# The gates of chunks 2 to 5 moved from the end of the opening to the middle of chunk 0

## The chip, the cores and the metric

The kernel runs on one core of a Trainium2 chip. The metric is the device time of one execution in microseconds (us); the median of a kernel's runs is what is compared. A profile is of one further execution, and gives its span: the time from the first to the last instruction.

## The reference

An mLSTM layer (a recurrent attention with an input, a forget and an output gate) over 4 batches of 8 heads, 768 positions and 40 values a head is followed by a gated feed-forward network of 320 inputs, 1536 inner columns and 320 outputs on the 3072 tokens. All is float32.

```
for t in range(S):                                   # 768 positions
    m_new  = max(f_gate[t] + m, i_gate[t])
    f_stab = exp(f_gate[t] + m - m_new); i_stab = exp(i_gate[t] - m_new)
    C = f_stab * C + i_stab * outer(v[t], k[t]); n = f_stab * n + i_stab * k[t]
    y[t] = sigmoid(o_gate[t]) * (C @ q[t]) / max(|n . q[t]|, 1)
x   = y as [4 * 768, 8 * 40]
out = (sigmoid(x @ w_gate) * (x @ w_val)) @ w_out
```

## The kernel before, in words

The 768 positions are six chunks of 128. A unit is one chunk of one batch (all 8 heads), so there are 24 units, (c, b). Inside a chunk the recurrence is written as attention: a unit's decay tile `d` of 128 x 8 x 128 is loaded from a small scratch row in DRAM, spread over the partitions (L219), turned into exponentials on ScalarE (L226, eight pieces, one for each head, in chunks 0 and 1), masked on POOL (L235), multiplied with the scores `s` (L427) and then with the values (`av`, L452). From chunk to chunk the state `cst` is carried: `in` (L447) reads it, `cs` (L500) adds to it through ScalarE copies (L512) and two VectorE sums (L517). The unit's result is divided by its denominator (L454 to L477) and transposed into `xh` and `xl`, the high and low parts of the feed-forward input of its chunk.

**Gates.** The gates of all 32 rows (batch times head) are rows of 768 numbers on 32 partitions. `gates_of(c0, c1)` makes the sums and maxima of chunks c0 to c1-1, all on VectorE: a running sum of the forget gates that starts anew in each chunk (L184), a difference (L185), for each chunk a running maximum `mg` and the value `mend` carried to the next chunk (L171, L172), and a last difference (L189). After each maximum SyncE stores `mg` to the scratch row `mscr` of its chunk (L173). Chunk 0's gates stand at the head of the opening and chunk 1's a little later in it; the call `gates_of(2, NCH)`, event g1, is for chunks 2 to 5: eleven VectorE operations (L184, L185 and L189 on 32 x 512, four L171 on 32 x 128, four tiny L172) and four stores. What they make is turned by TensorE: event h1 transposes the differences (`ptg`, four small L195) and VectorE copies them out as `at` (L197); event k1 transposes the last difference (`ptg` again), ScalarE takes its exponential `dec` (L199), and one more matmul and three VectorE operations spread it as `cdec` (L207 to L213).

**Feed-forward.** A tile (c, j, t0, t1) is inner column block j (12 of 128 columns) on 128 x (t1 - t0) tokens of chunk c. Its float32 products are made of high and low parts: 16 matmuls `pg` (L532 to L537) give gate and value in two PSUM tiles; then tanh on ScalarE (`sg`, L539), the product on VectorE (L540), a copy `gh` on ScalarE (L543), the remainder `gl` on VectorE (L544); the down matmuls `po` (L554 to L556) run one tile later. In chunk 0 the blocks 0 to 3 are done first on two batches, then on the other two (256 columns each), and blocks 4 to 11 on all four (512 columns).

**Weights.** They arrive as 64-bit words and are decoded during chunk 0, block by block: ScalarE (L259), VectorE (L264, L265, L269, tile `dc`), a high part on ScalarE (`wh` L294, `w` L297, `oh` L299) and a low part on POOL (`wl` L304, `w` L308, `ol` L310). SyncE issues nearly every load in one queue, in the program's order.

**Order.** Every step has a number in a table, `pos`; steps are recorded in the order of these numbers, and a feed-forward tile has its place in units of one full tile, so that 4.6 is shortly after block 4 of chunk 0. The framework's scheduler then orders each engine's instructions under the dependencies. Two things bind it: events of kind g, h and k are `pinned`, that is ordered behind the opening's last instruction on each engine; and `tc.issue_after(ins)` orders an engine's following instructions behind `ins`. PSUM tiles of the attention part share two banks of tag "pa": a tile that is to take a bank waits until the one before it there was read.

## Time and profile before

| | |
|---|---|
| runs | 572.92, 571.94, 572.35 us; median 572.35 |
| span of the profiled execution | 569.9 us; the median of the runs is 2.45 us above it, and the page gives no other time for the profiled execution |
| TensorE matmul busy | 546.7 us (96%), 3587 matmuls |
| VectorE / ScalarE / POOL busy | 319.5 us (56%) / 232.2 us (41%) / 162.2 us (28%) |
| DMA | 72.27 MB, mean 127 GB/s |

In the page's rows PE is TensorE, PEld its weight loads, DVE VectorE, ACT ScalarE, SP SyncE. In a list by time, the columns are start, time until the last of the group ended, engine, line, operation, output<-inputs, shape, count, and in brackets how long the engine had been idle and what ended that. A list of waits has engine and line, what it waited for, microseconds in total, times, longest. A table of windows has the window, its length, busy time of PE, PEld, DVE, ACT and POOL with counts, the granted TensorE clock (1.00 is full speed), the DMA engines' mean busy share and what they moved in GB/s.

### The profile page before, as it was taken

To read this page: it belongs to the slowest core of one execution; us is meant where nothing else is said; L and a number is where in the kernel's file an instruction comes from. 1 tells how busy PE (TensorE), PEld (TensorE's weight loads), DVE (VectorE), ACT (ScalarE), POOL (GpSimd) and SP (SyncE) were. 2 spreads that over 40 slices of the span, in tenths; PEclk is the share of its full clock that TensorE was granted. 3 is DMA by queue.
4 is the path that set the end of the run, shared out by engine and by line. 5 is a ranking of instruction groups with operands and counts; after the bars stand their busy time and mean duration, and the time that the engine had idled before them with its cause. 6 is when DMAs were issued, how large, how long until landed. Compare 5 with 4: busy or idle time off the path is not lost.

```text
span 569.9 us, 9906 instructions
## 1 busy us (share of the span) xinstructions
PE 546.7 (96%) x3587; PEld 497.0 (87%) x3587; DVE 319.5 (56%) x739; ACT 232.2 (41%) x581; POOL 162.2 (28%) x231
## 2 busy tenths in 40 slices
PE   8667999999999999999999999999999999999997
PEld 7565988788899999998888888888888888999996
DVE  5788878895755645555555544545543545432322
ACT  5285657754443442352243241433342332232322
POOL 5567646575420241311322310332210210000000
PEclk9789999999999999999999999999999999999999
DMA  9797747242674947354666544685644824010000
GB/s 197 193 240 185 202 123 192 93 115 54 169 173 119 183 103 182 100 147 125 167 125 156 132 141 129 149 171 124 140 125 134 206 56 121 4 47 2 24 2 23
DMA packets 131641, 72.27 MB, mean 127 GB/s; under 512 B 103113, under 2 KB 120777, under 8 KB 131593
## 3 DMA queue, kind: packets, MB, share of 16 engines
q1 hardware_dynamic: 130504, 71.39, 50.6%
q8 instruction: 28, 0.46, 0.3%
q10 hardware_dynamic: 1088, 0.26, 0.2%
q14 instruction: 21, 0.16, 0.1%
HBM read 56.95 MB, written 14.68 MB: 126 GB/s over the span
## 4 chain that ended last, share of the span: by engine, by line
PE 85%; DVE 7%; ACT 3%; issue 2%; POOL 2%; POOLq 0%; DVEq 0%; ACTq 0%
PE pg L532 34%; PE po L554 7%; PE po L556 7%; PE po L555 7%; PE av L452 6%; PE pg L534 6%; PE pg L537 6%; PE in L447 2%; PE s L434 2%; PE pt L373 2%; PE xt L488 2%; PE cs L500 2%; PE s L426 1%; DVE dc L264 1%; ACT d L226 1%
## 5 line engine op out<-in xcount | busy, mean ns | idle before, releaser
L539 ACT ACTIVATE sg<-pg 128x256 f32<-128x256 f32 (+1 forms) x103 | 48.3, 469 | 174.3 <-PE pg L537 174.2
L540 DVE SCALAR_TENSOR_TENSOR sg<-sg,pg 128x256 f32<-128x256 f32 (+1 forms) x103 | 53.9, 524 | 113.9 <-ACT sg L539 110.6
L532 PE MATMUL pg<-xh,wl 128*128 128x256 f32 (+1 forms) x412 | 111.1, 342 | 1.2 <-POOL wl L304 1.2
L532 PE MATMUL pg<-xh,wh 128*128 128x256 f32 (+1 forms) x412 | 110.9, 343 | 0.4 <-DVE sg L540 0.4
L532 PE MATMUL pg<-xl,wh 128*128 128x256 f32 (+1 forms) x412 | 108.7, 339 | 0.0
L556 PE MATMUL po<-oh,gl 128*128 128x320 f32 x288 | 93.0, 323 | 0.0
L554 PE MATMUL po<-oh,gh 128*128 128x320 f32 x288 | 92.3, 321 | 0.4 <-ACT gh L543 0.4
L555 PE MATMUL po<-ol,gh 128*128 128x320 f32 x288 | 92.4, 321 | 0.0
L544 DVE TENSOR_TENSOR gl<-sg,gh 128x256 fp32r<-128x256 f32 (+1 forms) x103 | 59.6, 579 | 35.5 <-ACT gh L543 34.9
L532 PEld LDWEIGHTS pg<-xh,wl 128*128 128x128 f32 x412 | 70.9, 191 | 8.5 <-POOL wl L304 1.4
L532 PEld LDWEIGHTS pg<-xh,wh 128*128 128x128 f32 x412 | 70.9, 191 | 5.8 <-DVE sg L540 0.6
L532 PEld LDWEIGHTS pg<-xl,wh 128*128 128x128 f32 x412 | 69.3, 190 | 6.6
L543 ACT ACTIVATE gh<-sg 128x256 fp32r<-128x256 f32 (+1 forms) x103 | 51.7, 502 | 47.7 <-DVE sg L540 47.7
L554 PEld LDWEIGHTS po<-oh,gh 128*128 128x128 f32 x288 | 54.5, 189 | 2.0 <-ACT gh L543 0.6
L555 PEld LDWEIGHTS po<-ol,gh 128*128 128x128 f32 x288 | 54.4, 189 | 1.3
L556 PEld LDWEIGHTS po<-oh,gl 128*128 128x128 f32 x288 | 54.2, 188 | 0.5 <-DVE gl L544 0.2
L534 PE MATMUL pg<-xh,w 128*128 128x256 f32 (+1 forms) x206 | 52.9, 332 | 0.7 <-POOL v L139 0.4
L537 PE MATMUL pg<-xl,w 128*128 128x256 f32 (+1 forms) x206 | 53.1, 331 | 0.0
L452 PEld LDWEIGHTS av<-v,d 128*128 128x128 f32 x352 | 46.8, 191 | 2.2 <-DVE d L427 0.6
L452 PE MATMUL av<-v,d 128*128 128x41 f32 x352 | 45.5, 269 | 0.4 <-DVE d L427 0.3
L508 POOL TENSOR_TENSOR cst<-cst,cdec 120x246 f32<-120x246 f32 (+1 forms) x32 | 16.0, 519 | 98.9 <-PE in L447 98.9
L235 POOL TENSOR_SCALAR_AFFINE_SELECT d<-d 128x1024 f32<-128x1024 f32 x22 | 24.2, 1101 | 50.1 <-ACT d L230 46.0
(128 smaller groups left out, 834.5 us busy)
## 6 DMA issues: line engine op xcount, KB each, us to landing
d<-mscr SPq DMA_DIRECT2D x22, 512.0 KB
ks<-scr SPq DMA_DIRECT2D x16, 360.0 KB
qs<-scr SPq DMA_DIRECT2D x16, 360.0 KB
k<-in_k_dram SPq DMA_DIRECT2D x24, 160.0 KB
v<-in_v_dram SPq DMA_DIRECT2D x24, 160.0 KB
o<-in_o_gate_dram SPq DMA_DIRECT2D x24, 160.0 KB
st_o<-in_moe_w_out_dram SPq DMA_DIRECT2D x12, 320.0 KB
out_dram<-ob SPq DMA_DIRECT2D x24, 160.0 KB
```

Of the source, the lines that this page charges most:

```text
L235: nc.gpsimd.affine_select(out=d, in_=d, pattern=[[0, H], [1, L]], compare_op=ALU.is_ge, fill=0.0, base=0, channel_multiplier=-1)
L452: nc.tensor.matmul(pv[:, h, :], dm[u][:, h, :], vt[u][:, h, :], start=True, stop=True)
L532: nc.tensor.matmul(pg[n], w[n][:, a, fs], x[c][:, a, n0:n1], start=(i + a == 0), stop=False)
L534: nc.tensor.matmul(pg[n], w2[n][:, fs], xh[c][:, 2, n0:n1], start=False, stop=False)
L537: nc.tensor.matmul(pg[n], w2[n][:, fs], xl[c][:, 2, n0:n1], start=False, stop=True)
L539: nc.scalar.activation(sg, pg[0], AF.Tanh, scale=0.5)
L540: nc.vector.scalar_tensor_tensor(sg, sg, 1.0, pg[1], ALU.add, ALU.mult)
L543: last = nc.scalar.activation(gh[u][:, :nt], sg, AF.Copy)
L544: E('gl0' if c == 0 else 'gl').tensor_tensor(gl[u][:, :nt], sg, gh[u][:, :nt].bitcast(F32), ALU.subtract)
L554: nc.tensor.matmul(po[t], g1[:, ts], oh[:, j, :], start=(j == 0), stop=False)
L555: nc.tensor.matmul(po[t], g1[:, ts], ol[:, j, :], start=False, stop=False)
L556: nc.tensor.matmul(po[t], g0[:, ts], oh[:, j, :], start=False, stop=(j == NF - 1))
```

## The change

The number of event g1 goes from 0.599 to 4.6, and its instructions are bound behind the VectorE remainder (`gl`, L544) of the feed-forward tile recorded last, here block 4 of chunk 0. Nothing is added to or taken from the computation.

```
-        ... 'w29': 13.171, 'g1': 0.599, 'h1': 5.3, 'k1': 5.5, ...
+        ... 'w29': 13.171, 'g1': 4.6, 'h1': 5.3, 'k1': 5.5, ...
@@ ffn_up
-        E('gl0' if c == 0 else 'gl').tensor_tensor(gl[u][:, :nt], sg, gh[u][:, :nt].bitcast(F32), ALU.subtract)
-        return last
+        lastv = E('gl0' if c == 0 else 'gl').tensor_tensor(gl[u][:, :nt], sg, gh[u][:, :nt].bitcast(F32), ALU.subtract)
+        return last, lastv
@@ emit
-            last = ffn_up(*tiles[kk])
+            last, lastv = ffn_up(*tiles[kk])
...
-                gates_of(2, NCH)
+                with tc.issue_after(lastv.ins):
+                    gates_of(2, NCH)
```

The scheduler makes of it the following orders. In the rows the running maxima and sums (L171, L184) are listed as SCALAR_TENSOR_TENSOR; `gin` is the tile of both gates, `dc_0_405` and `dc_1_415` are output weight blocks 0 and 1 in decoding.

VectorE at the end of the opening, before (L184, L185, three L171 and three L172 stand in a row ahead of this piece):

```order
L264 TENSOR_SCALAR dc_0_405<-dc_0_405 128x320
L171 SCALAR_TENSOR_TENSOR mg<-gin,mend 32x128
L264 TENSOR_SCALAR dc_1_415<-dc_1_415 128x320
L265 TENSOR_SCALAR dc_0_405<-dc_0_405 128x320
L265 TENSOR_SCALAR dc_1_415<-dc_1_415 128x320
L269 SCALAR_TENSOR_TENSOR dc_0_405<-st_o_139,dc_0_405 128x320
L269 SCALAR_TENSOR_TENSOR dc_1_415<-st_o_382,dc_1_415 128x320
L197 COPY at<-ptg_2_453 128x32
L172 TENSOR_TENSOR mend<-gin,mg 32x1
L189 TENSOR_TENSOR gin<-mend,mg 32x512
L540 SCALAR_TENSOR_TENSOR sg_0_0_474<-sg_0_0_474,pg_0_0_0_457 128x256
```

and now, directly behind the second unit's `xl`:

```order
L491 TENSOR_TENSOR xl_344<-xt_1_359,xh_343 128x3x128
L264 TENSOR_SCALAR dc_0_405<-dc_0_405 128x320
L265 TENSOR_SCALAR dc_0_405<-dc_0_405 128x320
L264 TENSOR_SCALAR dc_1_415<-dc_1_415 128x320
L269 SCALAR_TENSOR_TENSOR dc_0_405<-st_o_139,dc_0_405 128x320
L265 TENSOR_SCALAR dc_1_415<-dc_1_415 128x320
L197 COPY at<-ptg_2_453 128x32
L269 SCALAR_TENSOR_TENSOR dc_1_415<-st_o_382,dc_1_415 128x320
L540 SCALAR_TENSOR_TENSOR sg_0_0_474<-sg_0_0_474,pg_0_0_0_457 128x256
```

The eleven gate operations are gone from here; the decoding and the copy `at` of chunk 1's gates follow `xl` at once.

VectorE in the middle of chunk 0, from the remainder of block 4 to that of block 5, before (`o_0_398`, `t_1_0` and `x_0` belong to unit (1, 0); `dc_6_1230` is output weight block 6):

```order
L544 TENSOR_TENSOR gl_4_0_1045<-sg_4_0_1041,gh_4_0_1044 128x512
L265 TENSOR_SCALAR dc_3_1185<-dc_3_1185 128x256
L265 TENSOR_SCALAR dc_6_1230<-dc_6_1230 128x320
L454 TENSOR_TENSOR t_1_0_1053<-t_1_0_1053,av_0_1055 128x328
L269 SCALAR_TENSOR_TENSOR dc_3_1185<-st_3_911,dc_3_1185 128x256
L467 TENSOR_SCALAR den_0_1065<-t_1_0_1053 128x8
L471 SCALAR_TENSOR_TENSOR o_0_398<-o_0_398,t_1_0_1053 128x320
L468 SCALAR_TENSOR_TENSOR den_0_1065<-t_1_0_1053,den_0_1065 128x8
L269 SCALAR_TENSOR_TENSOR dc_6_1230<-st_o_929,dc_6_1230 128x320
L469 RECIPROCAL den_0_1065<-den_0_1065 128x8
L477 TENSOR_TENSOR x_0_1070<-o_0_398,den_0_1065 128x320
L540 SCALAR_TENSOR_TENSOR sg_5_0_1123<-sg_5_0_1123,pg_0_5_0_1106 128x512
```

Behind that piece stood L197, the copy `at`. Now, the later part of the same stretch (ahead of it, from `gl_4` on, stand L184, L185, two L171 and two L172, the unit's denominator and `x`, and the two L517):

```order
L171 SCALAR_TENSOR_TENSOR mg<-gin,mend 32x128
L540 SCALAR_TENSOR_TENSOR sg_5_0_1123<-sg_5_0_1123,pg_0_5_0_1106 128x512
L172 TENSOR_TENSOR mend<-gin,mg 32x1
L197 COPY at<-ptg_6_1130 128x128
L171 SCALAR_TENSOR_TENSOR mg<-gin,mend 32x128
L359 COPY qk_1_1136<-pt_1_1_1143 120x256
L172 TENSOR_TENSOR mend<-gin,mg 32x1
L544 TENSOR_TENSOR gl_5_0_1127<-sg_5_0_1123,gh_5_0_1126 128x512
L189 TENSOR_TENSOR gin<-mend,mg 32x512
L362 TENSOR_TENSOR qbd_1_1137<-qk_1_1136,bmask 80x256
L264 TENSOR_SCALAR dc_6_1230<-dc_6_1230 128x320
```

The gates are threaded between the unit's operations, and the decoding of block 6 has moved from both sides of `gl_4` to behind L189.

TensorE at the same place, before (`po_0_914` and `po_0_915` are the outputs of batches 2 and 3; `pt_1_1_1148` is the third transposed piece of unit (1, 1), `ptg_6_1174` the second turning of the gates):

```order
L357 MATMUL pt_1_1_1143<-ident,k_1_555 120x128
L556 MATMUL po_0_914<-oh,gl_4_0_1045 128x320
L554 MATMUL po_0_915<-oh,gh_4_0_1044 128x320
L555 MATMUL po_0_915<-ol,gh_4_0_1044 128x320
L556 MATMUL po_0_915<-oh,gl_4_0_1045 128x320
L357 MATMUL pt_1_1_1148<-ident,q_1_554 80x128
L357 MATMUL pt_1_1_1148<-ident,k_1_555 80x128
L532 MATMUL pg_0_6_0_1196<-xh_343,wh_98 128x512
L195 MATMUL ptg_6_1174<-ident,gin 128x32 x4
```

and now (the same tiles, with the outputs called 899 and 900):

```order
L357 MATMUL pt_1_1_1148<-ident,q_1_554 80x128
L555 MATMUL po_0_899<-ol,gh_4_0_1029 128x320
L357 MATMUL pt_1_1_1148<-ident,k_1_555 80x128
L556 MATMUL po_0_899<-oh,gl_4_0_1030 128x320
L554 MATMUL po_0_900<-oh,gh_4_0_1029 128x320
L555 MATMUL po_0_900<-ol,gh_4_0_1029 128x320
L556 MATMUL po_0_900<-oh,gl_4_0_1030 128x320
L532 MATMUL pg_0_6_0_1196<-xh_343,wh_98 128x512 x2
L532 MATMUL pg_0_6_0_1196<-xh_343,wl_99 128x512 x2
L195 MATMUL ptg_6_1174<-ident,gin 128x32 x4
```

The third piece moved forward by four matmuls, and by the program's dependencies it now takes the PSUM bank that the copy `at` (L197) must first have read; before, it took one that ScalarE had read. The second turning, which waits for L189 in both, moved back by three feed-forward matmuls. On SyncE the four stores of `mg` moved from behind the load of unit (1, 2)'s `d` to behind the loads of unit (1, 3)'s k and v, ahead of the load of output weight block 7.

More of the change, by code (lines that the diff above doesn't have):

```diff
@@ L857, in mlstm_then_gated_ffn_kernel @@
         ends[ins.engine] = ins
-    last = None
+    last = lastv = None
     def emit(p, kind, kk):
-        nonlocal last
+        nonlocal last, lastv
         c, b = divmod(kk, B)
         if kind == "up":
-            last = ffn_up(*tiles[kk])
+            last, lastv = ffn_up(*tiles[kk])
         elif kind == "down":
```

2 rows, old and new, of the table PARAM are left out of this document.

## The prediction

> **What bounds the kernel now.** I read the page first, for the engine that carries the span, then the waits and the rows by time at the two places between which the gates move.
>
> ```profile
> PE 546.7 (96%) x3587; PEld 497.0 (87%) x3587; DVE 319.5 (56%) x739; ACT 232.2 (41%) x581; POOL 162.2 (28%) x231
> PE   8667999999999999999999999999999999999997
> PE 85%; DVE 7%; ACT 3%; issue 2%; POOL 2%; POOLq 0%; DVEq 0%; ACTq 0%
> ```
>
> TensorE sets the end: 85% of the chain of waits is its work. The 40 slices (14.2 us each) show where it is not full: the second to fourth, 14 to 57 us, the end of the opening. What is won there moves the end; what stops TensorE later is lost one for one. Differences below 0.2% (1.1 us) a measurement of this kernel cannot tell from none.
>
> The waits from 29 to 47 us, and VectorE's rows there:
>
> ```profile
> PE pt L357 <- DVE at L197: 3.0, 1, 3.0
> ACT oh L299 <- DVE dc L269: 2.1, 1, 2.1
> ACT wh L294 <- DVE dc L269: 1.9, 2, 1.7
> ```
>
> ```profile
> 29.10 1.73 DVE L184 TENSOR_TENSOR_SCAN gin<-mg,gin 32x512 f32<-32x512 f32 x1
> 30.87 1.04 DVE L185 TENSOR_TENSOR gin<-gin 32x512 f32<-32x512 f32 x1
> 31.95 1.34 DVE L171 TENSOR_TENSOR_SCAN mg<-gin,mend 32x128 f32<-32x128 f32 x1
> 33.51 0.47 DVE L171 TENSOR_TENSOR_SCAN mg<-gin,mend 32x128 f32<-32x128 f32 x1
> ...
> 36.90 0.17 DVE L197 COPY at<-ptg 128x32 f32<-128x32 f32 x1
> ...
> 37.17 1.39 DVE L189 TENSOR_TENSOR gin<-mend,mg 32x512 f32<-32x512 f32 x1
> ...
> 42.11 1.20 DVE L265 TENSOR_SCALAR dc<-dc 128x512 int32<-128x512 int32 x1
> ...
> 43.56 1.48 DVE L269 SCALAR_TENSOR_TENSOR dc<-st,dc 128x512 int32<-128x512 int32 x1
> ```
>
> The gates fill VectorE from 29.1 to 35, and TensorE waits 3.0 us for the small copy `at` that stands behind them. The same L171 takes 0.47 or 1.34.
>
> **The gain at the opening.** Rows of ScalarE, SyncE, POOL and TensorE:
>
> ```profile
> 31.71 1.10 ACT L259 ACTIVATE dc<-st_o 128x320 f32<-128x320 f32 x2
> ...
> 36.60 0.87 ACT L299 ACTIVATE oh<-dc 128x320 fp32r<-128x320 f32 x2 [2.13 <-DVE dc L269]
> ...
> 38.00 2.44 ACT L226 ACTIVATE d<-d,at 128x128 f32<-128x128 f32 x8
> ```
>
> ```profile
> 32.62 0.69 SPq L219 DMA_DIRECT2D d<-mscr  x1
> ```
>
> ```profile
> 41.75 1.27 POOL L235 TENSOR_SCALAR_AFFINE_SELECT d<-d 128x1024 f32<-128x1024 f32 x1
> ...
> 43.32 1.16 POOL L362 TENSOR_TENSOR qbd<-qk,bmask 120x384 f32<-120x384 f32 x1
> 45.78 2.98 POOL L304 TENSOR_TENSOR wl<-dc,wh 128x512 fp32r<-128x512 f32 x2 [1.29 <-ACT wh L294]
> ```
>
> ```profile
> 33.88 0.25 PE L195 MATMUL ptg<-ident,gin 32*128 32x32 f32 x1 [1.42 <-ACT cst L512]
> ```
>
> With the gates gone, `at` follows its transpose at 33.88 + 0.25 = 34.15 in place of 36.90: 2.75 us, the upper end of the gain. Decoding starts when ScalarE's first piece is there (31.71 + 0.55), so `oh` no longer waits. What is late next is the load of unit (0, 3)'s `d`, issued at 32.62. No row shows its landing. ScalarE used it at 38.00 straight after other work, so it had landed by then. The page's k, v and o (160 KB each, ahead in the queue) and this 512 KB at the 245 GB/s of the window row further down are 4.05 us: 36.7 by estimate. I take 37.4. So ScalarE's eight exponentials, and `gh` and the decoding queued behind them, gain only 0.6 us. But POOL, whose `ol` now starts at about 34.5, is free when they end: its mask runs at 40.0 in place of 41.75 and its qbd at 42.4 in place of 43.32. VectorE's L265 and L269, which took 1.20 and 1.48 beside them, then run nearer to the 0.4 to 0.7 that such operations take alone, and end at 42.9 to 43.9 in place of 45.04. The high part, `wl` (45.78) and the first matmuls on it follow: 1.2 to 2.1 us earlier. I take **1.6 us**, ends 0.5 (the load alone decides, VectorE and POOL meet as before) and 2.75. From 50 us on TensorE has work at every step, so this reaches the end, unless it is given back.
>
> **The loss in mid chunk 0.**
>
> ```profile
> PE s L426 <- DVE d L427: 0.8, 1, 0.8
> PE av L452 <- DVE d L427: 0.3, 1, 0.3
> ```
>
> ```profile
> 85.84 1.20 DVE L264 TENSOR_SCALAR dc<-dc 128x320 f32<-128x320 f32 x1 [0.41 <-ACT dc L259]
> 86.96 0.68 DVE L544 TENSOR_TENSOR gl<-sg,gh 128x512 fp32r<-128x512 f32 x1
> ...
> 90.80 0.69 DVE L540 SCALAR_TENSOR_TENSOR sg<-sg,pg 128x512 f32<-128x512 f32 x1
> ```
>
> ```profile
> 90.43 0.43 PE L195 MATMUL ptg<-ident,gin 32*128 32x32 f32 x4
> ...
> 93.11 0.27 PE L357 MATMUL pt<-ident,q 128*80 128x128 f32 x1
> ...
> 93.73 0.43 PE L195 MATMUL ptg<-ident,gin 32*128 32x32 f32 x4
> ```
>
> The first fence is all that TensorE waited between 76 and 112 us: 1.1 us. Times here are in the clock of before. From the end of `gl_4` (about 87.6) to the copy `at` (about 91.4) VectorE had 3.8 us of work. Now four decoding operations leave this stretch (estimate 1.4) and the two L517 (1.1) and most of the gates come: L184, L185, three L171, three tiny L172. By the opening's rows that is 1.73 + 1.04 + 3 x 0.47 + 3 x 0.15 = 4.6; were L185 like `gl_4` (0.68, as many columns) and L184 in proportion 1.3, 3.8. Sum 7.3 to 8.1. Against that, the L264 and L265 of block 6 no longer stand around `gl_4`, which then ends at about 85.6. `at` is done at 93.0 to 94.0. TensorE now comes to the third `pt` at about 91.9 (before at 93.11, less four matmuls of 0.15 and the 0.3 us wait of `av`, which the earlier decoding removes) and stands until then: 1.1 to 2.1 us, taken 1.2, near the lower end, because POOL's low parts of block 3, which could slow these operations, stand earlier too. Behind `at` come L171, L359, L172, `gl_5` and L189, 2.2 to 2.9 us; TensorE needs 1.9 us from `pt` to the second `ptg`: a second wait of 0.3 to 1.0, taken 0.5. **Loss 1.7 us**, ends 0.3 and 3.1. While L171 and L189 are late, SyncE's queue stands too: behind the stores wait unit (1, 3)'s o, output block 7, unit (2, 0)'s q and the next weights.
>
> ```profile
> L173 SPq DMA_DIRECT2D mscr<-mg x5: 339/406/665, 24.7 to 64.6; - x5
> ```
>
> ```profile
> 104.26 2.54 POOL L304 TENSOR_TENSOR wl<-dc,wh 128x512 fp32r<-128x512 f32 x2
> ```
>
> The first of these `wl` is done near 105.5 and used by TensorE's third matmul of block 8 near 106.6, 1.1 us of slack; since TensorE is as late as the decoding, I cost this at nothing. At their old place the stores cost SyncE four times 0.41; the loads behind them start 1.6 us earlier, which is what lets block 5's decoding come sooner. The 0.3 us wait of `av` and about 0.5 of the 0.8 us wait of the scores (now L427 stands ahead of the L265 before it) go: **gain 0.8**, ends 0 and 1.1. The stores' first user, the load of unit (2, 0)'s d, stands behind all of these loads in SyncE's queue and loses nothing.
>
> The sum is -1.6 + 1.7 - 0.8 = -0.7 us: a span of 569.2. The median lies 2.45 above the span of before; I add the same: 571.65.
>
> On contention: the first L171 took 1.34 beside POOL's mask and 0.47 alone, so the gates' price depends on POOL. The Trainium skill, "GPSIMD Engine Reference", section Key points, says that GpSimd shares its SBUF interfaces with VectorE, so that VectorE operations with two SBUF inputs or in a two-port mode are slowed. The trace agrees (1.34 against 0.47); with all gates slowed the loss would be 0.8 us more than with none.
>
> On the clock, in four windows of TensorE's granted clock:
>
> ```profile
> 17.02:20.43 3.41, 1.24 (x6) 0.49 (x5) 3.38 (x5) 0.28 (x1) 1.53 (x2) 1.00 0.31 97
> 20.43:23.85 3.42, 3.42 (x19) 3.41 (x18) 2.45 (x10) 0.63 (x1) 0.78 (x2) 0.50 1.04 239
> ...
> 34.08:37.50 3.42, 0.42 (x3) 0.19 (x2) 3.32 (x13) 1.29 (x5) 0.34 (x1) 1.00 1.01 245
> 37.50:40.91 3.41, 3.08 (x15) 2.99 (x15) 1.85 (x4) 3.41 (x13) 2.87 (x4) 0.50 0.95 176
> 40.91:44.32 3.41, 1.76 (x14) 1.49 (x12) 3.23 (x5) 2.50 (x7) 3.35 (x4) 1.00 0.84 245
> 44.32:47.74 3.42, 2.04 (x8) 1.30 (x9) 3.21 (x7) 2.21 (x5) 2.13 (x3) 1.00 0.43 129
> ```
>
> A window with 0.42 or 1.24 us of matmuls was followed by one at half clock, one with 1.76 was not. Now TensorE has some 2 us in 34.08 to 37.50, so block 1's gate and value matmuls should run at full clock. That wins nothing: the down matmuls behind them wait for `gh` at 40. But the next window, 37.50 to 40.91, then holds only about 1.3 us of work.
>
> **The rivals.**
> - *The load decides.* `d` lands as late as 38.0 and VectorE meets POOL as before: gain 0.5. -0.5 + 1.7 - 0.8 = +0.4: 572.75. For it: DMA share 1.01 in that window. Against: POOL is free earlier.
> - *The gates fit in.* Loss at its lower end: -1.6 + 0.3 - 0.8 = -2.1: 570.25. For it: VectorE is busy only 56% overall and had idle time on both sides of this place (next rival). Against: `at` is in front of TensorE by its order.
> - *Slower: the decoding falls behind.* Blocks 6 and 7 now stand behind L189 and the stores; ScalarE's queue carries `oh` and L259 for them ahead of the next tanh. If block 4's weight L269 comes more than 1.1 us later than TensorE itself, TensorE stops at `wl`; with VectorE 5 us behind it stands 3.9 in place of 1.7, and keeps the 0.5 us score wait: -1.6 + 3.9 - 0.3 = +2.0: 574.35. Against: idle time of VectorE behind that place, in these rows of before 2.9 us, takes up part.
>
> ```profile
> 95.94 0.77 DVE L264 TENSOR_SCALAR dc<-dc 128x320 f32<-128x320 f32 x1 [1.46 <-ACT dc L259]
> ...
> 104.68 0.69 DVE L540 SCALAR_TENSOR_TENSOR sg<-sg,pg 128x512 f32<-128x512 f32 x1 [1.41 <-ACT sg L539]
> ```
>
> - *Half clock.* 1.3 us of work in a window is between 1.24 and 1.76; if the next runs at half clock, its 1.76 us of matmuls cost up to 1.5 more: +0.8: 573.15. The Trainium skill, "TensorE: Matmul & The Clock Gate", Part 1, says that a free-running window of about 3.4 us that is idle halves the clock. By it a partly used window would not, though the row at 17.02 did; then the sum stands.
> - That nothing moves is excluded: the orders show all eleven operations elsewhere.
>
> **How the numbers follow.** The forecast has 0.38; it is within 0.2% if it comes as worked out, but its own spread of a microsecond gives 0.15 to faster, 0.22 to same, 0.01 to slower. The load 0.14 (same), the gates fit in 0.20 (faster), the decoding 0.21 (slower), half clock 0.07 (0.06 same, 0.01 slower). Together faster 0.35, same 0.42, slower 0.23. The range, 569.9 to 574.3, reaches from just under the second rival to just under the third.
>
> **What would show it.** The 3.0 us wait for `at` near 37 falls under 1; the exponentials start near 37.4; `wl` starts near 44; TensorE waits for L197 and for L189 between 88 and 98, 1.7 us together; the score wait near 109 shrinks. Wrong would be: no wait at `pt` or `ptg`, a wait for `wl` in block 8, or exponentials still at 38.

## The result: 0.7% slower, and the profile after

| | before | after |
|---|---|---|
| median of 13 runs each | 572.35 us (569.86 to 576.15) | 576.56 us (574.56 to 581.68) |
| ratio | | 1.0073, 95% interval 1.0046 to 1.0100 |
| span of the profiled execution | 569.9 us | 574.7 us |
| time of the profiled execution itself | not given | 576.47 us |
| mean granted clock of the profiled execution | 0.988 | 0.985 |

The forecast was 571.65, range 569.9 to 574.3. The time is above the range and on the other side.

From the page of after, the busy row, the two rows by slice (14.4 us each) and the shares of the chain:

```profile
PE 548.9 (96%) x3587; PEld 496.3 (86%) x3587; DVE 319.1 (56%) x739; ACT 232.3 (40%) x581; POOL 161.7 (28%) x231
PE   8559999899999999999999999999999999999997
PEclk9787999999999999999999999999999999999999
PE 82%; DVE 6%; ACT 4%; POOL 2%; DMA 2%; issue 2%; SPq 1%; POOLq 0%; DVEq 0%; ACTq 0%
```

The work is the same: VectorE has 0.4 us less in all. TensorE's busy time is 2.2 us longer; most of that is matmuls at half clock, seen in the fourth slice, where PEclk says 7 (the mean clocks above make it 1.8 us). The eighth slice, 101 to 115 us, has fallen to 8.

To find where the 4.8 us arise, the end of the last gate or value matmul (`pg`, L537) of each feed-forward tile is compared; these ends are start plus duration of rows of the list by time.

| end of `pg` of | before | after | difference |
|---|---|---|---|
| chunk 0 block 0, first half | 32.46 | 31.40 | -1.06 |
| block 1, first half | 41.79 | 37.51 | -4.28 |
| block 2, first half | 54.77 | 54.77 | 0.00 |
| block 3, second half | 75.89 | 75.90 | +0.01 |
| block 5 | 90.36 | 90.70 | +0.34 |
| block 6 | 98.07 | 99.38 | +1.31 |
| block 8 | 112.18 | 115.89 | +3.71 |
| block 11 | 132.97 | 137.06 | +4.09 |
| chunk 1 block 0, its first tile | 144.80 | 149.30 | +4.51 |
| last tile | 563.93 | 568.82 | +4.89 |

The opening won 1 to 4 us at its first two tiles and had nothing left at the third. Nearly all of the loss, 4.5 of 4.9 us, lies between 82 and 150 us. Below, **the middle** is the time from the end of block 3 to the end of chunk 1's first tile (the expectations call that tile chunk 1's second block): 68.91 us before, 73.40 after, +4.5. **The opening** is the time from the end of block 0 to that of block 2: 22.31 and 23.37. Both are read from one profile for each kernel. The middle repeats well (before's order of the middle gave 68.8 and 69.0 in two other kernels); the opening does not, as the account of the prediction below shows.

The opening of after, by time, rows of VectorE, TensorE, ScalarE and POOL:

```profile
33.28 0.18 DVE L197 COPY at<-ptg 128x32 f32<-128x32 f32 x1
33.52 0.33 PE L357 MATMUL pt<-ident,q 128*120 128x128 f32 x1 [0.43 <-DVE at L197]
37.21 2.44 ACT L226 ACTIVATE d<-d,at 128x128 f32<-128x128 f32 x8 [2.15 <-DMA d<-mscr]
39.73 1.09 POOL L235 TENSOR_SCALAR_AFFINE_SELECT d<-d 128x1024 f32<-128x1024 f32 x1 [2.11 <-ACT d L226]
42.17 1.52 POOL L362 TENSOR_TENSOR qbd<-qk,bmask 120x384 f32<-120x384 f32 x1 [1.02 <-ACT qk L361]
43.64 1.44 POOL L304 TENSOR_TENSOR wl<-dc,wh 128x512 fp32r<-128x512 f32 x1
43.74 2.93 PE L426 MATMUL s<-qbd,qk 120*128 120x384 f32 x4 [1.42 <-POOL qbd L362]
```

Every step comes as early as predicted, down to `wl`. But four score matmuls take 2.93 us (before: 1.56). The windows of the granted clock, with the columns of the prediction's table, say why:

```profile
36.44:39.85 3.41, 1.07 (x10) 0.86 (x8) 0.00 (x0) 2.64 (x9) 1.30 (x3) 1.00 1.00 184
39.85:43.26 3.41, 2.31 (x6) 1.54 (x6) 3.23 (x6) 3.16 (x9) 2.33 (x3) 0.50 0.87 280
43.26:46.68 3.42, 2.94 (x5) 1.73 (x6) 3.18 (x4) 1.27 (x4) 1.83 (x2) 0.50 0.52 159
46.68:50.09 3.41, 3.41 (x15) 3.15 (x15) 3.11 (x7) 1.06 (x3) 2.06 (x2) 0.50 0.53 154
```

While the load of `d` is waited for, TensorE has 1.07 us of work in a window, and the three windows behind it run at half clock; before, one such window ended at 40.91.

The middle of after, VectorE and ScalarE by time, and TensorE's waits behind 60 us:

```profile
93.37 0.27 DVE L197 COPY at<-ptg 128x128 f32<-128x128 f32 x1
...
98.28 0.49 DVE L269 SCALAR_TENSOR_TENSOR dc<-st_o,dc 128x320 int32<-128x320 int32 x1
...
102.35 0.68 DVE L540 SCALAR_TENSOR_TENSOR sg<-sg,pg 128x512 f32<-128x512 f32 x1
...
104.89 0.68 DVE L544 TENSOR_TENSOR gl<-sg,gh 128x512 fp32r<-128x512 f32 x1
...
110.72 1.39 DVE L264 TENSOR_SCALAR dc<-dc 128x320 f32<-128x320 f32 x1
112.03 0.55 DVE L427 TENSOR_TENSOR d<-s,d 128x384 f32<-128x384 f32 x1
```

```profile
98.81 0.47 ACT L299 ACTIVATE oh<-dc 128x320 fp32r<-128x320 f32 x1 [1.81 <-DVE dc L269]
99.18 0.48 ACT L259 ACTIVATE dc<-st_o 128x320 f32<-128x320 f32 x1
99.56 1.40 ACT L259 ACTIVATE dc<-st 128x512 f32<-128x512 f32 x2
100.86 0.59 ACT L539 ACTIVATE sg<-pg 128x512 f32<-128x512 f32 x1
```

```profile
PE s L426 <- DVE d L427: 2.4, 2, 1.5
PE pt L357 <- DVE at L197: 0.9, 1, 0.9
PE pt L373 <- DVE xl L491: 0.7, 1, 0.7
PE pg L532 <- ACT sg L539: 0.5, 2, 0.4
```

`at` ends at 93.64, within the predicted 93.0 to 94.0. Behind it block 6's output weights are decoded 9 us later than before (L269 at 98.28; it was at 89.30). ScalarE waits 1.81 us for that with block 6's tanh behind it in its queue, so that the block's remainder `gl` ends 6.2 us after its matmuls (99.38 to 105.57), before 3.5. At the end TensorE waits 1.52 us to write the next scores, until L427 has read the last ones, in place of 0.76; ahead of L427 stands an L264 of 1.39.

### The profile page after: what moved, and what is told of

Read it like the earlier page. It is cut to its first block, busy times and chain, and to the rows that moved or that the text cites. A ratio compares the mean times of both kernels' runs of the same rounds, so it can differ in the third digit from the quotient of the medians.

```text
span 574.7 us, 9915 instructions
## 1 busy us (share of the span) xinstructions
PE 548.9 (96%) x3587; PEld 496.3 (86%) x3587; DVE 319.1 (56%) x739; ACT 232.3 (40%) x581; POOL 161.7 (28%) x231
## 4 chain that ended last, share of the span: by engine, by line
PE 82%; DVE 6%; ACT 4%; POOL 2%; DMA 2%; issue 2%; SPq 1%; POOLq 0%; DVEq 0%; ACTq 0%
PE pg L532 33%; PE po L554 7%; PE po L556 7%; PE po L555 7%; PE av L452 6%; PE pg L534 6%; PE pg L537 5%; PE in L447 2%; PE s L434 2%; PE pt L373 2%; PE s L426 2%; PE cs L500 2%; PE xt L488 1%; ACT d L226 1%; PE mb L643 1%
## 5 line engine op out<-in xcount | busy, mean ns | idle before, releaser
L539 ACT ACTIVATE sg<-pg 128x256 f32<-128x256 f32 (+1 forms) x103 | 48.2, 468 | 174.3 <-PE pg L537 174.3
L540 DVE SCALAR_TENSOR_TENSOR sg<-sg,pg 128x256 f32<-128x256 f32 (+1 forms) x103 | 54.0, 524 | 113.8 <-ACT sg L539 110.6
L556 PE MATMUL po<-oh,gl 128*128 128x320 f32 x288 | 93.6, 325 | 0.0
L544 DVE TENSOR_TENSOR gl<-sg,gh 128x256 fp32r<-128x256 f32 (+1 forms) x103 | 59.0, 573 | 37.9 <-ACT gh L543 37.3
L537 PE MATMUL pg<-xl,w 128*128 128x256 f32 (+1 forms) x206 | 52.9, 331 | 0.0
```

Source lines behind the costliest of these rows:

```text
L537: nc.tensor.matmul(pg[n], w2[n][:, fs], xl[c][:, 2, n0:n1], start=False, stop=True)
L539: nc.scalar.activation(sg, pg[0], AF.Tanh, scale=0.5)
L540: nc.vector.scalar_tensor_tensor(sg, sg, 1.0, pg[1], ALU.add, ALU.mult)
L544: lastv = E('gl0' if c == 0 else 'gl').tensor_tensor(gl[u][:, :nt], sg, gh[u][:, :nt].bitcast(F32), ALU.subtract)
L556: nc.tensor.matmul(po[t], g0[:, ts], oh[:, j, :], start=False, stop=(j == NF - 1))
```

## The experiments

Times of profiles are single executions; ratios are against before, with 95% intervals.

**Is it the middle?** e1 leaves the gates at the opening and makes them again at 4.6 (its outputs are not the reference's); e2 makes them at 2.6; e3 turns them a full tile later.

```
e1  + pos["g", 2] = 0.599   and   + elif kk == 2: gates_of(2, NCH)   ahead of the new call
e2  'g1': 4.6 -> 2.6
e3  'h1': 5.3 -> 6.3, 'k1': 5.5 -> 6.5
```

> The gates of chunks 2 to 5 are computed twice: at the opening as before, and again in mid chunk 0 as after (the second pass works in place on the first one's result, so the outputs are not the reference's; the instructions and their sizes are the same). This prices the two ends of the move apart. Theory A (the opening gave nothing: the load of unit (0,3)'s d at 37.2 and three half-clock windows took back what the early at copy won; the whole 4.8 us arose between 82 and 167 us): the kernel stands where the changed one stands, 4 to 5 us above the kernel before in the span (573.9 to 575), ratio about 1.007 to 1.009, its opening ends at 54.8 as before, and block 8 of chunk 0 ends 3 to 4 us later than before. Theory B (the opening did gain about 1.6 in the usual run and mid chunk 0 loses more than the profile of one run shows): it is slower than the changed kernel by 1 to 2 us, ratio 1.010 to 1.012.

> The gates are tied behind the latest feed-forward remainder at place 2.6 (about 65 us) in place of 4.6; the turning stays at 5.3 and 5.5. The opening is that of the changed kernel. Theory A (the loss is of the place: at 88 to 100 us VectorE is busy 11.5 of 12 us, TensorE waits for the at copy and the decoding falls behind; from 64 to 76 VectorE is busy 9.0 of 12): the mid loss falls from 4.8 to 0 to 1.5 us, span 569.5 to 571.5, ratio 0.999 to 1.003. Rival C (any 5.6 us of VectorE work in chunk 0 after the opening costs the same, wherever it stands): span 573 to 575, ratio about 1.007. If the opening did gain (theory B), 567.5 to 569, ratio 0.995 to 0.998.

> The changed kernel with the two turnings (h1, k1) recorded one feed-forward block later, at 6.3 and 6.5, gates at 4.6 as in the change. Theory D (the waits of TensorE for L197 and L189 start the loss: 0.91 us at 93.7, then the ScalarE and VectorE queues behind it): the wait for L197 falls under 0.3 and the loss to 1 to 3 us, span 571 to 573, ratio 1.001 to 1.005. Theory E (the VectorE work itself delays the decoding and the score products; the wait for L197 is only its first sign): the wait goes, but block 8 still ends 3 us or more later than before, span 573.5 to 575, ratio 1.005 to 1.009.

e1: 1.0197 (1.0161 to 1.0233), middle 79.2, in which a 3.4 us wait for a tanh near 135 us and one window at half clock behind it are a place of its own; the opening stayed at 22.6. That is above both forecasts. At block 8, ahead of that place, it stands 4.4 us behind before, so the middle alone is enough to make the kernel slower. e2: 1.0048 (1.0024 to 1.0071), between the forecasts of theory A and rival C; middle 70.2, but from block 2 of the second half to block 8, which takes in the new place, 3.0 more than before (after: 3.7). e3: 1.0083 (1.0055 to 1.0112), middle 73.8. The wait for `at` was gone and others had come: `pt_cdec` behind `dec` 1.3 us, `s` behind `cdec` 1.2, `pg` behind a tanh 0.9. So taking away the wait at `at`, which the prediction priced, saves nothing by itself.

**Why does the opening win nothing?** e4 issues unit (0, 3)'s `d` load ahead of its k, v and o. e5 puts 16 spare matmuls of 128 x 256 on TensorE behind block 1's `pg`, where the hole is in after (from 37.5 us; in e5 they ran from 39.5 to 42.2), with the orders of after.

```
e4  - load_unit(u // B, u % B)
    + dmat_load(u // B, u % B) if u == B - 1 else None; load_unit(u // B, u % B)
    ...
e5  + for _ in range(16): nc.tensor.matmul(po0[:, :256], wh[0][:, 0, :P], xh[0][:, 0, :256], start=True, stop=True)
```

> The changed kernel with the load of unit (0,3)'s d issued ahead of that unit's q, k, v and o, where it doesn't queue behind v's wait for its buffer. Theory F (that load held ScalarE's exponentials at 37.2 in the changed kernel): the load lands at about 32, the exponentials start at 34.5 to 35.5, ScalarE's wait of 2.1 and TensorE's wait of 2.5 us for gh at 40.0 fall under 0.7, and the opening (end of block 2's pg, 54.8) ends 1 to 2.5 us earlier, span 572.2 to 573.7 with the mid loss left in. Theory G (the clock decides: after the idle stretch the windows are at half clock whatever the load does, or the decoding of block 1 and 2 is as late): the exponentials start early, but the opening ends within 0.5 us of 54.8, span 574.2 to 575.2.

> The changed kernel with 16 more matmuls of 128x256 (0.12 us each, into a PSUM bank that the next product overwrites) in TensorE's idle stretch from 37.4 to 40.0 us of the opening; every engine's order is otherwise that of the changed kernel. Theory H (the clock: the changed kernel's opening ran at half clock for 10.2 us from 39.85 on, in two other profiles of the same opening 6.8 and 10.2 us, against 3.4 us in two profiles of the old opening): the half clock there falls to 0 to 3.4 us, and the time from the end of block 0 to that of block 2 falls from 22.5 to 23.6 (three profiles) to 20.5 to 22.0; the whole is 1 to 2.5 us faster than the changed kernel, ratio to before 1.002 to 1.006. Rival I (block 2 waits for its decoded weights, POOL's w at 54.0 and VectorE before it, and TensorE's clock only fills that time): the half clock goes but the stretch stays at 22.3 or more, ratio 1.006 to 1.009.

e4: 1.0131 (1.0098 to 1.0165). The load landed at 32.55, 4.6 us earlier, and the scheduler then put the eight exponentials ahead of ScalarE's state copies L512, for which TensorE waits:

```profile
37.39 0.25 PE L195 MATMUL ptg<-ident,gin 32*128 32x32 f32 x1 [4.96 <-ACT cst L512]
```

The opening took 23.9, and the middle 73.9 with a window at half clock at 95.6. The time is above both forecasts. Since the order changed with the load, this run doesn't show what the load alone is worth. e5: 1.0088 (1.0058 to 1.0117); its opening took 21.9, 1.5 less than after's, but the middle 74.3, with a window at half clock at 112. Block 2 ended at 54.32, 0.45 earlier than in after. Profiles of after's opening without spare work differ by more than that (below), so it isn't shown that the spare work helped even where it stood.

**How much of it is the gates' time?** e6 leaves L184 and L185 at the opening and the rest at 4.6. e7 has the rest tied behind block 0's L540 (0.61) instead, so that no gate is in the middle. e8 is e7 with 20 spare matmuls.

```
e6, e7  + gates_of(2, NCH, "a")                                 # L184, L185, at 0.599
e6      + with tc.issue_after(lastv.ins): gates_of(2, NCH, "b")   # the others, at 4.6
e7, e8  + with tc.issue_after(mul[0].ins): gates_of(2, NCH, "b")  # the others, at 0.61
```

> The changed kernel with the first two of the eleven operations (L184 and L185, 1.97 us of VectorE in mid chunk 0) back at the opening, the other nine in mid chunk 0. From the end of block 3 (second half, 75.9) to that of the second block of chunk 1 (144.8) the kernel before takes 68.9 us, the changed one 73.4, the early one 70.2, the late-turned one 73.8. Theory E (VectorE paces mid chunk 0, so what stands there costs nearly its own length): the stretch falls by 1.5 to 2.5, to 71 to 72, ratio to before 1.002 to 1.006. Theory J (the chain behind the last difference L189, the at copy and their PSUM bank costs, not the amount): less than 0.7 us less than the changed kernel, ratio 1.006 to 1.009.

> The gates stay in the opening but in VectorE's two idle stretches there: L184 and L185 behind the second unit's xl (28.1 to 31.2 in the changed kernel), the maxima and L189 bound behind block 0's product L540 (35.9 to 40.0), so the decoding of output blocks 0 and 1 and the at copy come before them. Theory K (a place where VectorE waits costs nothing, and mid chunk 0 is what cost): the stretch from block 3 to chunk 1's second block is back at 68 to 69.5, the opening is that of the changed kernel, and the whole is the kernel before within 1.2 us (ratio 0.998 to 1.002); with the half clock of the changed opening nothing is won. Rival L (the maxima now delay gl of block 0, the decoding of block 1 and the score products): block 2 ends 1 to 2 us later than before, ratio 1.002 to 1.004.

> The kernel of the split opening with 20 more matmuls of 128x256 behind block 1's last pg, every other order the same. Theory H (clock): one to three half-clock windows fewer than the split opening, from block 0's end to block 2's 1 to 2.5 us less, ratio to before 0.994 to 0.998: faster than both kernels. Rival I (the decoded weights of block 2 decide): the same as the split opening within 0.6 us.

e6: 1.0056 (1.0034 to 1.0078), middle 71.6: with 2 us less of gates there it is 1.8 us less. But the scheduler also moved other rows: block 6's L269 starts 17.7 us behind the end of block 3, in after 22.4. e7: 1.0087 (1.0054 to 1.0120), and its middle still took 71.5, though it held no gate. This was unexpected: a middle without gates can be 2.6 us longer than before's. e8 repeats it: 1.0068 (1.0044 to 1.0092), middle 71.1, opening 21.6 against 24.8 in e7; its time is far above the forecast of 0.994 to 0.998. What e7 and e8 share with after is that the scheduler, once an early step is moved, orders everything behind it anew. They don't share the place: e7 is only 0.3 us behind before at block 8 and 2.2 at block 11, after 3.7 already at block 8, and block 6's decoding stands in e7 where it stood before. So e7 raises the question of the order; after's own order is priced by the next runs.

**Order or work?** From here on each engine's instructions are tied in a written order, which separates the two.

```
+ for x, y in zip(line, line[1:]):                     # line: an engine's instructions in the chosen order
+     tc.add_manual_dep(y, x.name, link, reason="order")
e9   after's order on all engines, but the gates at the opening
e10  before's order; gates threaded into the middle as in after, second turning moved back
e11  before's order; gates put into VectorE's idle gaps from 68 to 79 us
e12  before's order; in the opening, decoding of blocks 0 and 1, `at`, L540 and L359 ahead of the maxima
e13  e12 with 16 spare matmuls behind block 1's `pg`;   e14  before's order with 16 behind the first `ptg`
```

> The order of the changed kernel on every engine, held by issue edges from each instruction to the next, but the gates and their stores at the opening as before (and the few decoding steps that the change moved ahead of them there). The stretch from the end of the two-batch blocks (75.9 before) to chunk 1's second block took 68.9 us before and 73.4 after. Theory E (VectorE's added 5.6 us pace mid chunk 0; the new order is only its dress): the stretch falls to 68.5 to 70, the whole is before within 1.2 us, ratio 0.998 to 1.003. Theory M (the table of numbers fits the old order; what costs is that the scheduler recast the decoding, the score products and the transposes around the gates, as in the split opening, which lost 2.5 us in this stretch with no gate in it): 71.5 to 73.5, ratio 1.004 to 1.008.

> The order of the kernel before on every engine, held by issue edges, and only the eleven gate operations threaded into VectorE's row behind block 4's gl, with the four stores, the second turning (ptg, dec, cdec) moved behind block 6's pg, where the last difference is ready. Theory E: VectorE has no idle time from 84 to 94 us, so block 5's and 6's operations come 4 to 5 us later; the stretch takes 72 to 75.5 us, ratio 1.005 to 1.011. Theory M: 69 to 71, ratio 0.999 to 1.004.

> The order of the kernel before on every engine, held by issue edges, and only the eleven gate operations threaded into VectorE's idle times from 68 to 79 us (behind L540 and L544 of the last two-batch blocks, where it waits for ScalarE), the four stores behind the loads there. Theories E and M agree on the middle: the stretch stays at 68.9 within 0.7 (no order changed, no busy stretch lengthened). The opening then has the gates gone: from block 0's end to block 2's 20.5 to 22.3 us if that is worth anything with an unchanged order (22.3 before); ratio 0.995 to 1.000. If even here the middle grows by 1.5 or more, idle time of VectorE is no guide, ratio 1.002 to 1.006.

> The order of the kernel before on every engine, held by issue edges; only within the opening the decoding of output blocks 0 and 1, the at copy, block 0's product and the qk copy go ahead of the maxima (L171, L172) and L189, which then stand where VectorE waits for ScalarE (36 to 40 us); L184 and L185 stay where they were. Theory M: the middle as before, 68.9 within 0.7 (the split opening, with the scheduler's own order, took 71.5); opening 21 to 23 us from block 0 to block 2, ratio 0.996 to 1.002. Theory E says the same of the middle, so this run with the split opening's tells the order apart from the amount. If the stretch is 71 again, neither holds.

> The held split opening (e12) with 16 more matmuls of 128x256 behind block 1's last pg, where TensorE waits for gh; nothing else moved on any engine. In e12 the opening took 23.8 us from block 0's end to block 2's, with half clock in 36.2 to 39.6 and 43.0 to 49.9; the old opening takes 22.3 to 22.6 with 3.4 us of half clock (three profiles). Theory H (clock): at most 3.4 us of half clock from 34 to 50, the stretch 21 to 22.4, the middle 69.0 as in e12; ratio to before 0.995 to 0.9995, the fastest kernel so far. Rival I (POOL's qbd and the decoded w of block 2 set the end of the opening whatever the clock): 23.3 or more, ratio 0.999 to 1.003.

> The kernel before, its order held, with 16 more matmuls of 128x256 behind the transposed differences of chunk 1 (ptg), where TensorE waits 3.0 us for the at copy (34.1 to 37.1). Theory H: the half-clock window from 37.5 to 40.9 goes, block 1's products there run at full clock, and 0.3 to 1.2 us of the opening are won (22.3 to 21.1 to 22.0), ratio 0.997 to 1.000. Rival I: the half clock goes but POOL's qbd at 44.5 sets the next step as before, 22.3 within 0.3, ratio 0.999 to 1.001.

| | ratio (95%) | middle | opening |
|---|---|---|---|
| before | 1 | 68.9 | 22.3 |
| after | 1.0073 (1.0046 to 1.0100) | 73.4 | 23.4 |
| e9, new order without the gates | 1.0037 (1.0007 to 1.0067) | 71.6 | 22.5 |
| e10, old order with the gates in the middle | 1.0112 (1.0073 to 1.0150) | 75.0 | 23.5 |
| e11, old order, gates in idle gaps | 1.0073 (1.0034 to 1.0113) | 74.0 | 25.5 |
| e12, old order, changed in the opening | 1.0007 (0.9980 to 1.0035) | 69.0 | 23.8 |
| e13, e12 with spare work | 0.9993 (0.9955 to 1.0030) | 69.4 | 23.9 |
| e14, before with spare work | 0.9990 (0.9962 to 1.0017) | 68.8 | 23.1 |

The new order alone costs 2.7 us of the middle; putting the gates into it costs another 1.8, all of it by block 7, half of it the wait at `at` (0.91). e9's wait for the scores is that of after (first row; the second is before's):

```profile
110.79 0.70 PE L426 MATMUL s<-qbd,qk 80*128 80x256 f32 x2 [1.51 <-DVE d L427]
108.92 0.70 PE L426 MATMUL s<-qbd,qk 80*128 80x256 f32 x2 [0.76 <-DVE d L427]
```

With the old order held, the opening can be changed and the middle does not move (e12). But the old order is no place for the gates either: e10 and e11 lose 5 to 6 us in the middle, with two windows each at half clock behind new stops that end at 94 and 88 us. e10's longest stop:

```profile
94.06 0.47 PE L357 MATMUL pt<-ident,q 128*120 128x128 f32 x1 [2.19 <-ACT ct L512]
```

So the shares depend on what is put in first. In the old order the gates cost 6.1 us, and the new order, made for them, gives 1.6 back; without them it costs 2.7. The gaps that e11 filled are, in before's rows, waits of VectorE for the tanh or for `gh`, its reaction times in the chain tanh, L540, `gh`, `gl`; by e11's loss they were not spare time. And no version here is faster than before by more than its interval. e9, e10 and e12 came out in the middle as theory M, E and M had it. e13 went as its rival I; e14's opening came out longer than both forecasts.

**Which rows of the new order?** e15 (on e9) and e16 (on after) put block 6's decoding back in its old place: L264, L265, L269 on VectorE, the copy `oh` on ScalarE, POOL's order. e17 (on e9) and e18 (on after) leave the decoding and move block 6's evacuation (its tanh, L540, `gh`, `gl`, which read its `pg`) ahead of it.

```
e17, e18  ScalarE: L299, +L539, L259, L259, +L543, L259, ...   (L539 stood behind the three L259; L543 behind the next L299 and its L259)
          VectorE: L264, +L540, L213, L265, L269, +L544, L264, L264, ...
```

> The reorder-only kernel (e9: order of the changed kernel, gates at the opening), but output block 6's decoding back where it was: its L264 and L265 around block 4's gl, its L269 in the middle of unit (1, 0)'s denominator, ScalarE's oh copy behind block 3's w, POOL in its old order. In e9 it stood 6 us later (L269 at 95.5), and behind it block 7's decoding, ScalarE's copies and so the tanh and gh of blocks 6 and 7; TensorE then waited 1.5 us for the score product L427. Theory N (that displaced decoding is the order's cost): the stretch from the two-batch blocks to chunk 1's second block falls from 71.6 to 68.7 to 70, ratio 0.999 to 1.003. Rival O (the av block ahead of pg of block 5, the score products of unit (1, 0) or something later): 70.7 or more, ratio 1.002 to 1.005.

> The changed kernel's own order, held, with the gates in mid chunk 0 as in the change, and block 6's decoding put back ahead of and between them as in e15. Theory N: of the 4.5 us lost in the middle about 2.7 come back and the gates' own time of about 1.8 stays: stretch 70.3 to 71.8, ratio 1.002 to 1.005. Rival P (VectorE's row is so full there that what is taken from the decoding's delay is added to the gates' and the at copy's: the wait for at grows from 0.9 to about 2.3 and the rest stays): 72.5 to 74.5, ratio 1.005 to 1.010.

> The kernel of e9 (the new order without the gates in the middle; its stretch from the end of block 3's gate products to those of chunk 1's second block took 71.57 us, 68.91 before), with only block 6's evacuation moved ahead of decoding: on ScalarE its tanh (L539) directly behind the copy oh (L299) instead of behind three L259, and its gh (L543) ahead of the next L299; on VectorE its L540 and gl (L544) ahead of three L264 and two L265. In e9 block 6's gl ended 5.4 us after its products, 3.4 before. Theory Q (the order's cost begins where block 6's evacuation stands behind the decoding): gl ends 3.5 to 4.2 us after the products, the tanh and the chain of block 7 follow earlier, the score wait of 1.51 falls to 0.8 or less, and the stretch comes to 69.3 to 70.3. Theory R (the decoding itself is what is late for block 8; the evacuation had slack): what is put behind comes later, weights or scores are waited for, and the stretch stays at 71.2 to 72.5, with the gain at block 6 given back by block 8.

> The kernel after, its own order held, with the same four instructions moved ahead of decoding (block 6's tanh and gh on ScalarE, its L540 and gl on VectorE). In after gl ended 6.1 us after the products, the stretch took 73.40, TensorE waited 0.35 and 0.16 for the tanh and 1.52 for the scores. Theory Q: gl ends 3.5 to 4.5 us after the products, the waits for the tanh go, the score wait falls under 1, the stretch comes to 70.5 to 72, and the time to 1.003 to 1.006 of before. Theory R: the stretch stays at 73 to 74.5, the time at 1.007 to 1.010, because decoding for block 8 is 2 us later by then than it was.

e15: 1.0049 (1.0019 to 1.0079), middle 72.0; e16: 1.0100 (1.0066 to 1.0133), middle 75.6, with a window at half clock from 93.6. Neither is as short as theory N had it. The score wait did fall to 0.6 in e15, and a new one had come ahead of it, since the copy `oh` now stood ahead of ScalarE's copy `ct`:

```profile
PE pt L357 <- ACT ct L512: 1.5, 1, 1.5
PE pg L532 <- ACT sg L539: 1.3, 1, 1.3
PE s L426 <- DVE d L427: 1.0, 2, 0.6
```

From the end of block 6 to that of block 8 e15 took 13.9 us, e9 15.7 and before 14.1. So with the decoding in its old place the loss ahead of block 8 is gone; but TensorE came to block 6 1.2 us later than in e9, which gave the other engines that much more time, and from block 8 to block 11 e15 took 1.4 us more than e9, with a wait of 1.3 for a tanh.

e17: 1.0058 (1.0035 to 1.0080), middle 71.6, as e9 and as theory R had it. e18: 1.0084 (1.0052 to 1.0115), middle 72.7, 0.7 less than after and between the two theories. In both, `gl` ends 3.3 us after its matmuls, as it should, and the score wait is 1.5 as ever. So the late evacuation of block 6 was mostly slack. ScalarE and VectorE in e17 show what is not:

```profile
102.46 0.45 ACT L259 ACTIVATE dc<-st 128x256 f32<-128x256 f32 x1 [1.03 <-POOL ol L310]
102.81 2.44 ACT L226 ACTIVATE d<-d,at 128x128 f32<-128x128 f32 x8
105.16 0.61 ACT L294 ACTIVATE wh<-dc 128x512 fp32r<-128x512 f32 x1
105.68 0.57 ACT L539 ACTIVATE sg<-pg 128x512 f32<-128x512 f32 x1
...
109.08 1.39 DVE L264 TENSOR_SCALAR dc<-dc 128x320 f32<-128x320 f32 x1
110.39 0.55 DVE L427 TENSOR_TENSOR d<-s,d 128x384 f32<-128x384 f32 x1
```

and in before:

```profile
98.91 0.88 POOL L310 TENSOR_TENSOR ol<-dc,oh 128x320 fp32r<-128x320 f32 x1 [1.21 <-ACT oh L299]
99.82 0.45 ACT L259 ACTIVATE dc<-st 128x256 f32<-128x256 f32 x1 [0.99 <-POOL ol L310]
100.69 2.44 ACT L226 ACTIVATE d<-d,at 128x128 f32<-128x128 f32 x8
104.07 0.58 ACT L539 ACTIVATE sg<-pg 128x512 f32<-128x512 f32 x1
...
107.27 0.31 DVE L264 TENSOR_SCALAR dc<-dc 128x320 f32<-128x320 f32 x1
108.32 0.55 DVE L427 TENSOR_TENSOR d<-s,d 128x384 f32<-128x384 f32 x1
```

With block 6's decoding late, two output blocks are decoded in this stretch where there was one. The next L259 waits for POOL's second `ol` (101.50 in e17) and comes 2.6 us later; the exponentials, the copy `wh` and block 7's tanh queue behind it on ScalarE, the tanh 1.6 us later; then VectorE's L540, `gl`, an L264 that now runs beside POOL's `wl` and takes 1.39 in place of 0.31, and L427 (110.39, before 108.32). The rows show this chain. From the end of block 7 to that of block 8 e9 loses 1.6 us against before. That putting right this chain alone would save them isn't shown: in e15 the score wait at its end fell, but block 7's tanh came no earlier against the end of block 3 than in e9 (29.7 us, e9 29.5, before 28.2), and the repair disturbed another queue. The last 0.9 us of the order's 2.7, at block 11 and chunk 1's first tile, were not traced.

## Why the prediction was wrong, point by point

- *The opening, 1.6 us: next to none of it came.* The steps were right: `at` 33.3 to 33.5 (34.15 predicted), exponentials at 37.21 (37.4), the mask at 39.73 (40.0), qbd at 42.17 (42.4), `wl` at 43.64 (44), and the load was late next, as said. What failed there is the clock: the sum left half clock out and gave it a chance of 0.07 as a rival, because 1.3 us of work in a window was thought to be near the border; it was 1.07, and not one but three windows ran at half. One profile shows after's order with less of that: e18, where behind block 0 only 36.87 to 40.28 is at half clock:

```profile
33.45:36.87 3.42, 1.83 (x12) 1.20 (x12) 2.22 (x8) 2.92 (x12) 1.72 (x2) 1.00 0.99 242
36.87:40.28 3.41, 3.41 (x18) 3.38 (x18) 1.18 (x3) 3.41 (x11) 2.71 (x3) 0.50 0.98 204
40.28:43.69 3.41, 2.04 (x10) 1.29 (x8) 3.38 (x7) 2.17 (x8) 1.64 (x3) 1.00 0.77 225
```

  Its block 2 ended at 52.76, 2.0 us earlier than before. That is the best of five. The same opening order ended block 2 at 54.77 in after, 53.63 in e2, 55.85 in e3 and 54.54 in e16, with 10.2, 6.8, 10.2 and 13.7 us at half clock behind block 0. Before's opening order ended it at 54.77 in before, 53.35 in e1, 54.88 in e9, 55.26 in e15 and 54.54 in e17, with 3.4 us at half clock in four of them and 6.8 in e17. The means are 54.3 and 54.6: a gain of 0.3, less than the scatter of either five.
- *The wait in the middle, 1.7 us: the place was right, the size near.* `at` came in the predicted microsecond; the wait there was 0.91 (1.2 predicted) and the wait for the second turning was gone (0.5 predicted). The prediction's own terms for TensorE's arrival, 93.11 less four times 0.15 and 0.3, give 92.2 and not 91.9, which makes its wait 0.8 to 1.8. Its other terms give 1.4 us as the least loss (1.1 and 0.3); the lower end of 0.3, which a rival goes by, follows from none of them. Nor does 1.3 for L184 in proportion to L185: 1.73 x 0.68 / 1.04 is 1.1. In mid chunk 0 they took 1.21 and 0.76. e9 against after prices the gates in the new order at 1.8, e10 against before the gates in the old order at 6.1.
- *Small waits, a gain of 0.8: it became a loss.* The wait of `av` was gone, as predicted (0.3). The score wait was to shrink by 0.5 and doubled, 0.76 to 1.52.
- *"I cost this at nothing", of the decoding behind L189: this is the step that failed most.* It was checked against one user only, TensorE's third matmul of block 8 on `wl`, and there indeed no wait came. The new order that displaced this decoding costs 2.7 us of the middle with no gate in it (e9), 1.8 of them by block 8. By the rows the price was paid on queues: L259 behind POOL's `ol`, tanh behind `wh`, L427 behind L264. That this decoding is what costs the 1.8 rests on the rows and on e15's stretch from block 6 to block 8; no run got the time back. What the other 0.9 are is open.
- *From span to time:* 2.45 us were added; after's profiled execution shows 1.77 (576.47 against 574.7). It is a small term beside the others.
- *The rivals.* "The decoding falls behind", +2.0, had the right sign and in part the right cause, but the wrong place (a stop at `wl`), and half the size of the 4.2 measured. "The gates fit in" and the load as the sole limit fell.
- *Beside it all:* the sum priced the moved operations where they went. It did not price that the table's one number lets the scheduler order anew what was not moved. The order views showed block 6's decoding and the second turning elsewhere; they were read as helps.

## What to carry to other kernels

When a moved step makes a scheduler order the rest anew, follow each displaced instruction through the queue that it now stands in, to every user behind it, and not only to the engine that sets the end: here the new order cost 2.7 us before the moved step was even put into it. Test order apart from work: hold the new order without the moved step, and the old order with it. Run both, for the two need not add up: here the step cost 1.8 us in the new order and 6.1 in the old. And a stretch in which the clock drops is not read from one profile of each kernel. An idle gap of an engine that answers another is often the answer's own delay; look what ended the gap before filling it.

## What the hardware showed

**The clock's windows.** In all 20 profiles the granted clock changes only on a grid of 3.41 us, whose phase to the start differs from run to run. Set TensorE's matmul rows against it, with borders read off the same windows. At full clock 151 windows held less than 2.70 us of matmuls, and 56 of them were followed by half clock, among these all 32 with less than 1.53 us; of some 3000 windows with more than 2.70, none was. Out of half clock: 34 windows with less than 2.79 us busy were all followed by another at half clock; of 77 with more, 56 were followed by full clock. The Trainium skill, "TensorE: Matmul & The Clock Gate", Part 1, has the same free-running window of 3413 ns; by its table an idle window lowers the clock. Here a partly used one was enough, and the way back needed at least four fifths of one. So a stop that leaves a window more than 0.7 us short of work may be followed by half clock, and here one that left it 1.9 us short always was. The same opening order ended block 2 up to 3.1 us apart in five profiles (52.76 to 55.85). That this comes from where the grid lies is likely; it isn't shown, since the moments at which loads landed were not held fixed.

**Spare matmuls are no sure cure.** In e13 the half clock only came later (48.2 to 58.5 us), and in e14 too (43.9 to 50.7). The opening was 1.5 us shorter in e5 than in after and 3.2 shorter in e8 than in e7, but with no spare work at all it took 18.95 to 24.52 in the five profiles of after's order, so these differences prove nothing.
